# A weight maximum's matmul moved behind its diagonal, in a fused attention and two-layer expert kernel

## The chip, the cores and the metric

The kernel runs on one core of a Trainium2 chip. Its engines work in parallel, each through its own queue in a fixed order: TensorE (PE, matmuls), VectorE (DVE), ScalarE (ACT), GpSimd (POOL) and SyncE (SP, which issues most DMA transfers). They meet by semaphores. The metric is the device time of one execution in microseconds (us), as the median of several runs. Traces come from one further execution under the hardware profiler.

## The reference

Attention without softmax, then two mixture-of-experts layers in which each token goes to one expert.

```python
scores = (1 / S) * z @ z.T            # 4 batches, S = 2496, 64 features
x = u * (np.maximum(scores, 0) ** 2 @ v)          # 9984 tokens of 256

logits = x @ w_gate                   # 8 experts
e_idx = argmax(logits);  gate_w = softmax(logits)[e_idx]
for e in range(8):                    # first layer; eom = sigmoid(x @ w_output_gate)
    y[mask_e] = gate_w * eom[:, e] * (np.maximum(x[mask_e] @ w1[e], 0) @ w2[e])   # hidden 1024
# the second layer: the same with weights of its own and without eom
```

All of it is float32 at the interface.

## The kernel before

The kernel multiplies in float16 with two parts a number: a high part, and a low part that holds what the high part lost. A product is then three matmuls. Every weight matrix must be scaled by a power of two near its largest magnitude and split before it can be used. There are 32 weight matrices of 1 MB (two a layer and expert). The 16 of the first layer are split during attention, the 16 of the second layer during the first expert layer, and that is where the change is.

**The expert layer.** Tokens were scattered into regions by expert. The layer works on 85 tiles (slots) of 128 tokens. Its program is a list `order` of 170 items, written out when the program is built: `g1` items (first matrix and Relu, for one half of a pair of slots) and `g2` items (second matrix, for one slot). In the steady part a g1 and a g2 alternate. I call an item a step, and count from 0; from step 16 on the even ones are g1, the odd ones g2.

- `g1` (L1279): 24 matmuls into a PSUM tile `hp`; ACT does the Relu into the high part of the buffer HB (L1303), DVE makes HB's low part (L1304). There are two `hp` tiles, used in turn.
- `g2` (L1306): 24 matmuls into a PSUM tile `yp`; there are two of these too. `post1` (L1332) then takes the row maximum on DVE (`gm`, L1345) and a scale from it (`yg`), ACT makes the scaled high part (L1347), and DVE the low part (`rowb`, L1350). Every four slots the routing for the second layer follows in some twenty short DVE instructions and four scatters on POOL.

**The weights of the second layer.** `weight_pieces(..., offload=True)` (L392) returns a list of small pieces. From step 31 on, the end of a step takes the next piece; in the first steps it takes two, so that the list lasts exactly to the last of these steps (L1626 to L1631). A matrix has these pieces:

- `p0`, `p1`: the largest magnitude of the first and second half of the matrix, a DVE reduction of 128x1024 each (L427, L430). `p1` also puts the 128 partitions' maxima on a diagonal, `wd` (L436).
- `p1b`: appends the diagonal to the queue `wmq`. The next g2 takes it out and multiplies it by a matrix of ones (`wm_mm`, L384). The product stands in unused columns of that g2's `yp` tile and has all 128 maxima in every partition.
- `first`: `p2s` reduces that product to the maximum (`wy`, L450) and makes the scale `ws`. Then ACT scales half of the matrix in place and makes its high part (`phi`, L463 and L464), and POOL subtracts for the low part (`plo`, L471).
- `last`: `phi` and `plo` of the other half.
- `flush`: POOL issues the stores of the split halves (L477) and the load of the matrix after the next one (L402). There are two load buffers, `wstB`.

There are seven pieces a matrix, some of them empty, so a matrix takes seven steps, and the pieces of successive matrices fall on g1 and g2 in turn. The order on each engine is that in which this Python code calls the instructions; no scheduler changes it.

Of the kernel before, what the change touches and what calls it, by code (L numbers as in the profile page):

```python
# [27 lines left out]
def kernel(  # L28
# [15 lines left out]
    P = 128  # L44
    B, S, D = u.shape
# [334 lines left out]
        return pieces  # L380

    wmq = deque()

    def wm_mm(dst):  # L384
        st, dg = wmq.popleft()
        st["wm"] = dst
        T.matmul(dst, onesb, dg, start=True, stop=True)

# [3 lines left out]
    def weight_pieces(items, wst, wo, eng, offload):  # L392
        pend = []

        def flush():
            while pend:
                pend.pop(0)()
# [8 lines left out]
        def mk(k):  # L406
            i, e = items[k]
            w = wst[k % 2]
            st = {}
# [19 lines left out]
            def p1():  # L429
                V.tensor_reduce(st["m"][:, 1:2], w[:, H:], axis=AX.X, op=ALU.max, apply_absolute_value=True)  # L430
                if offload:
                    m1 = sm.tile([P, 1], F32, name=f"wx{i}_{e}", tag="wx")
                    dg = sm.tile([P, P], BF16, name=f"wd{i}_{e}", tag="fd", bufs=1)
                    tt(m1, st["m"][:, 0:1], st["m"][:, 1:2], ALU.max)
                    V.tensor_single_scalar(m1.bitcast(I32), m1.bitcast(I32), EXPM, ALU.bitwise_and)
                    V.tensor_scalar(dg, idn, m1, None, ALU.mult)  # L436
                    st["dg"] = dg
                    return
                st["m2"] = sm.tile([P, 2], F32, name=f"wr{i}_{e}", tag="wr")
                GP.partition_all_reduce(st["m2"], st["m"], P, bass.bass_isa.ReduceOp.max)  # L440

            def p1b():
                wmq.append((st, st["dg"]))

            def p2s():
                m1 = sm.tile([P, 1], F32, name=f"wy{i}_{e}", tag="wy")
# [49 lines left out]
                pass  # L496

            if offload:
                return (p0, p1, none, p1b, none, first, last)
            return (p0, p1), (p2s, lambda: phi(0), lambda: plo(0)), (lambda: phi(1), lambda: plo(1))  # L500

        ms = [mk(k) for k in range(len(items))]

        none = (0.0, lambda: None)
        if offload:
            pieces = [(0.0, lambda: w_load(0)), none, none, (0.0, lambda: w_load(1)), none]
            for m in ms:
                pieces += [(0.0, flush)] + [(0.0, f) for f in m]
                pieces[-len(m) - 1 : -len(m) + 1] = [(0.0, lambda p0=m[0]: (flush(), p0()))]
            return pieces + [(0.0, flush)]  # L510

        cost = (1.14, 1.14), (0.8, 0.67, 1.2), (0.67, 1.2)

# [3 lines left out]
        pieces = [(0.0, lambda: w_load(0)), none, none, none] + part(0, 0) + [(0.0, lambda: w_load(1)), none]  # L517
        for k in range(len(items)):
            last = part(k, 2)
# [786 lines left out]
    def g2(m, s):  # L1306
        e = eoff2.pop((m, s))
        i, h, _ = hslot.pop((m, s))
        hfree.append((i, h))
        yp = ps.tile([P, 512], F32, name=f"yp{m}_{s}", tag="a")  # L1310
        if wmq:
            wm_mm(yp[:, D : D + P])
        for f in range(FC):
            rh = wreg(e, arena0 + W2O + f * 4 * D)
            rl = wreg(e, arena0 + W2O + f * 4 * D + 2 * D)
            hi = T.lower_ap(HB[i][:, 0, f, h * P : h * P + P], for_matmul_weights=True)
            lo = T.lower_ap(HB[i][:, 1, f, h * P : h * P + P], for_matmul_weights=True)
            mm_reg(yp[:, :D], hi, reg_ap(rh, D, W2F), f == 0, False)
            mm_reg(yp[:, :D], hi, reg_ap(rl, D, W2F), False, False)
            mm_reg(yp[:, :D], lo, reg_ap(rh, D, W2F), False, f == FC - 1)  # L1320
        return yp

    lgq = deque()
# [229 lines left out]
    for m in range(2):  # L1553
# [42 lines left out]
        touched2 = False  # L1596
        for at, o in enumerate(order):
            kind, s = o[:2]
            if wload:
                wload.popleft()()  # L1600
            if kind == "g1":
# [73 lines left out]
```

## Time and profile before

| | |
|---|---|
| median of 3 runs (lowest to highest) | 1708.35 us (1705.81 to 1709.58) |
| the profiled execution | 1695.75 us |
| its span, first to last instruction | 1693.9 us |
| PE busy | 1627.4 us, 96% of the span |
| DVE busy | 1103.2 us, 65% |
| ACT busy | 934.2 us, 55% |
| POOL busy | 391.4 us, 23% |
| mean granted PE clock | 0.988 of full speed |

An instruction is busy from its start to its end. A time of idleness stands with the instruction that ended it, together with what released that instruction ("<-DVE wd L436": the semaphore came from DVE's instruction on `wd`, line 436). Engines other than the one that decides may be idle at no cost. The granted clock is given as a share of 2.4 GHz; its other level is half of that.

Attention ends some 700 us into the span. The first expert layer's steps follow (its first hp matmul starts at 704.0 us), the part with the weight pieces being from about 800 to 1160 us, and the second expert layer runs from about 1230 us to the end.

### The profile page before, as it was taken

The page shows a single profiled execution, that of the slowest core. Times are in us where ns is not written, and L with a number is a line of the kernel's source. Part 1 is how long each engine was busy: PE and PEld are TensorE (multiplying, and loading weights), DVE is VectorE, ACT ScalarE, POOL GpSimd, SP SyncE. Part 2 cuts the span into 40 slices and gives each one's busy share as a digit, 9 for nine tenths or more (in the row PEclk, how much of TensorE's full clock was granted, in tenths as well). Part 3 has the DMA queues.
Part 4 walks back from the last instruction along what each step waited for, and adds up shares of the span by engine and source line. Part 5 has one row for each costly group of instructions (what it writes and reads, how often), then busy time and mean ns, then how long its engine had stood idle before and what let it go on. Part 6 is the DMA issues. An engine that isn't in the chain of part 4 may idle for free. (4 is left out here: it accounts for less than half of the span.)

```text
span 1693.9 us, 41656 instructions
## 1 busy us (share of the span) xinstructions
PE 1627.4 (96%) x15668; PEld 1350.4 (80%) x15668; DVE 1103.2 (65%) x2805; ACT 934.2 (55%) x1082; POOL 391.4 (23%) x385
## 2 busy tenths in 40 slices
PE   8999999999999999989899899889989999999998
PEld 6777677767776777778788778789878888889997
DVE  8799899989999898656666766675463222222221
ACT  8898899889988998422344344443132222222221
POOL 1011111121111221111344344443121111111113
PEclk9999999999999999999999999999999999999999
DMA  5441643363534446962685568653892222222210
GB/s 147 122 110 44 192 101 90 115 202 101 133 99 143 140 138 183 286 167 62 179 186 167 159 157 175 159 141 87 248 275 60 67 51 51 51 51 52 52 33 30
DMA packets 289518, 212.05 MB, mean 125 GB/s; under 512 B 232297, under 2 KB 261358, under 8 KB 284976
## 3 DMA queue, kind: packets, MB, share of 16 engines
q1 hardware_dynamic: 268432, 144.51, 35.5%
q0 software_dynamic: 20896, 64.89, 11.6%
q8 instruction: 134, 2.20, 0.5%
q14 instruction: 56, 0.46, 0.1%
HBM read 92.80 MB, written 69.30 MB: 96 GB/s over the span
## 5 line engine op out<-in xcount | busy, mean ns | idle before, releaser
L1041 PEld LDWEIGHTS <-p 128*128 128x128 f16 (+1 forms) x4644 | 443.8, 98 | 105.3 <-issue 40.2
L1151 PE MATMUL yp<-W2R,HB 128*128 x4080 | 485.4, 278 | 0.1
L1151 PE MATMUL hp<-xt,W1R 128*128 128x256 f16 (+1 forms) x5088 | 475.4, 252 | 9.4 <-DMA xt<-region 3.9
L1151 PEld LDWEIGHTS <-HB 128*128 128x128 f16 x4080 | 403.8, 100 | 88.7 <-issue 36.4
L1304 DVE SCALAR_TENSOR_TENSOR HB<-hp,HB 128x1024 f16<-128x1024 f32 x170 | 207.8, 1223 | 385.2 <-ACT HB L1303 384.8
L1151 PEld LDWEIGHTS <-W1R 128*128 x5088 | 413.0, 98 | 46.1 <-issue 7.0
L1303 ACT ACTIVATE HB<-hp 128x1024 f16<-128x1024 f32 x170 | 173.4, 1021 | 246.3 <-PE hp L1151 236.4
L1041 PE MATMUL acc<-vhA,p 128*128 128x256 f16 (+1 forms) x2322 | 271.1, 273 | 3.6 <-DVE p L151 1.6
L1041 PE MATMUL acc<-vhB,p 128*128 128x256 f16 (+1 forms) x2322 | 270.6, 273 | 0.6 <-ACT acs L1051 0.6
L151 DVE TENSOR_TENSOR p<-r,p 128x1024 f16<-128x1024 f32 (+4 forms) x260 | 244.7, 954 | 36.6 <-ACT p L1006 33.8
L998 ACT ACTIVATE r<-s 128x1024 f32<-128x1024 f32 (+1 forms) x200 | 198.7, 994 | 56.2 <-PE s L987 48.0
L999 ACT ACTIVATE r<-r 128x1024 f32<-128x1024 f32 (+1 forms) x200 | 207.2, 1036 | 6.4
L654 POOL DMA_INDIRECT region<-rowb,pi x80 | 100.1, 1252 | 399.2 <-DVE pi L645 380.9
L1006 ACT ACTIVATE p<-r 128x1024 f16<-128x1024 f32 (+1 forms) x180 | 186.3, 1035 | 5.1
L1442 POOL DMA_INDIRECT out_dram<-rowb,oi x85 | 83.5, 983 | 348.0 <-ACT rowb L1441 342.4
L1347 ACT ACTIVATE rowb<-yp,yg 128x256 f16<-128x256 f32 x85 | 40.1, 472 | 223.2 <-DVE yg L167 187.4
L654 POOL DMA_INDIRECT region<-rowb,piq x85 | 85.0, 1000 | 208.3 <-DVE piq L641 64.7
L1441 ACT ACTIVATE rowb<-yp,cs 128x256 f32<-128x256 f32 x85 | 40.3, 474 | 143.2 <-PE yp L1151 136.3
L471 POOL TENSOR_TENSOR woB<-wstB,woB 128x1024 f16<-128x1024 f32 x32 | 68.1, 2133 | 100.6 <-ACT woB L464 100.5
L1350 DVE SCALAR_TENSOR_TENSOR rowb<-yp,yg,rowb 128x256 f16<-128x256 f32 x85 | 41.1, 483 | 54.5 <-ACT rowb L1347 53.8
L1345 DVE TENSOR_REDUCE gm<-yp 128x1 f32<-128x256 f32 x85 | 35.5, 418 | 27.5 <-PE yp L1151 27.4
L463 ACT ACTIVATE wstB<-wstB,ws 128x1024 f32<-128x1024 f32 x32 | 36.6, 1143 | 30.1 <-DVE ws L457 30.1
(266 smaller groups left out, 1159.1 us busy)
## 6 DMA issues: line engine op xcount, KB each, us to landing
wstA<-in_moe_w_dram SPq DMA_DIRECT2D x16, 1024.0 KB
wsplit<-woA SPq DMA_DIRECT2D x32, 512.0 KB
W1R<-wsplit SPq DMA_DIRECT2D x16, 1024.0 KB
W2R<-wsplit SPq DMA_DIRECT2D x16, 1024.0 KB
wstB<-in_moe_w_dram POOLq DMA_DIRECT2D x16, 1024.0 KB, 8.9
wsplit<-woB POOLq DMA_DIRECT2D x32, 512.0 KB, 4.8
u<-in_u_dram SPq DMA_DIRECT2D x16, 512.0 KB
vraw<-in_v_dram SPq DMA_DIRECT2D x3, 2432.0 KB
```

The source lines that it names most:

```text
L151: V.tensor_tensor(o, a, b, op)
L471: GP.tensor_tensor(lo, src, hi, ALU.subtract)
L654: d = GP.indirect_dma_start(reg[m], bass.IndirectOffsetOnAxis(ap=posi[:r, t : t + 1], axis=0), rows[:r, t, :], None, bounds_check=NROW - 1 ...
L998: A.activation(r[:, :, :W], s[:, :, :W], AF.Relu)
L999: A.activation(r[:, :, :W], r[:, :, :W], AF.Square, scale=2.0)
L1006: A.activation(p[:, 0, :, :W], r[:, :, :W], AF.Copy)
L1041: T.matmul(o, l, r, start=first and i == 0, stop=j == NT - 1 and i == len(mms) - 1, skip_group_check=True,)
L1151: T.add_instruction(mybir.InstMatmult(name=nc.get_next_instruction_name(), ins=[rhs, lhsT], outs=[T.lower_ap(o)], start_tensor_calc=start, ...
L1303: A.activation(hv, hpv, AF.Relu)
L1304: V.scalar_tensor_tensor(lv, hpv, 0.0, hv, ALU.max, ALU.subtract)
L1350: V.scalar_tensor_tensor(r16[:, q, D : 2 * D], yp[:, :D], yg, r16[:, q, :D], ALU.mult, ALU.subtract)
L1442: d = GP.indirect_dma_start(out, bass.IndirectOffsetOnAxis(ap=ot[:, q : q + 1], axis=0), y, None, bounds_check=N - 1, oob_is_err=False,)
```

## The change

```diff
--- before.py
+++ after.py
@@ -380,9 +380,10 @@
         return pieces
 
     wmq = deque()
+    at_item = [0]
 
     def wm_mm(dst):
-        st, dg = wmq.popleft()
+        _, st, dg = wmq.popleft()
         st["wm"] = dst
         T.matmul(dst, onesb, dg, start=True, stop=True)
 
@@ -434,13 +435,10 @@
                     tt(m1, st["m"][:, 0:1], st["m"][:, 1:2], ALU.max)
                     V.tensor_single_scalar(m1.bitcast(I32), m1.bitcast(I32), EXPM, ALU.bitwise_and)
                     V.tensor_scalar(dg, idn, m1, None, ALU.mult)
-                    st["dg"] = dg
+                    wmq.append((at_item[0] + 4, st, dg))
                     return
                 st["m2"] = sm.tile([P, 2], F32, name=f"wr{i}_{e}", tag="wr")
                 GP.partition_all_reduce(st["m2"], st["m"], P, bass.bass_isa.ReduceOp.max)
-
-            def p1b():
-                wmq.append((st, st["dg"]))
 
             def p2s():
                 m1 = sm.tile([P, 1], F32, name=f"wy{i}_{e}", tag="wy")
@@ -496,7 +494,7 @@
                 pass
 
             if offload:
-                return (p0, p1, none, p1b, none, first, last)
+                return (p0, p1, none, none, none, none, first, last)
             return (p0, p1), (p2s, lambda: phi(0), lambda: plo(0)), (lambda: phi(1), lambda: plo(1))
 
         ms = [mk(k) for k in range(len(items))]
@@ -504,10 +502,14 @@
         none = (0.0, lambda: None)
         if offload:
             pieces = [(0.0, lambda: w_load(0)), none, none, (0.0, lambda: w_load(1)), none]
-            for m in ms:
-                pieces += [(0.0, flush)] + [(0.0, f) for f in m]
-                pieces[-len(m) - 1 : -len(m) + 1] = [(0.0, lambda p0=m[0]: (flush(), p0()))]
-            return pieces + [(0.0, flush)]
+            steps = [list(m[:7]) for m in ms] + [[]]
+            for k, m in enumerate(ms):
+                steps[k][1] = lambda p1=m[1]: (flush(), p1())
+                if k:
+                    steps[k][0] = lambda lo=ms[k - 1][7], p0=m[0]: (p0(), lo())
+                steps[k] = [(0.0, f) for f in steps[k]]
+                pieces += steps[k]
+            return pieces + [(0.0, ms[-1][7]), (0.0, flush)]
 
         cost = (1.14, 1.14), (0.8, 0.67, 1.2), (0.67, 1.2)
 
@@ -1308,8 +1310,6 @@
         i, h, _ = hslot.pop((m, s))
         hfree.append((i, h))
         yp = ps.tile([P, 512], F32, name=f"yp{m}_{s}", tag="a")
-        if wmq:
-            wm_mm(yp[:, D : D + P])
         for f in range(FC):
             rh = wreg(e, arena0 + W2O + f * 4 * D)
             rl = wreg(e, arena0 + W2O + f * 4 * D + 2 * D)
@@ -1318,6 +1318,8 @@
             mm_reg(yp[:, :D], hi, reg_ap(rh, D, W2F), f == 0, False)
             mm_reg(yp[:, :D], hi, reg_ap(rl, D, W2F), False, False)
             mm_reg(yp[:, :D], lo, reg_ap(rh, D, W2F), False, f == FC - 1)
+        if wmq and at_item[0] >= wmq[0][0]:
+            wm_mm(yp[:, D : D + P])
         return yp
 
     lgq = deque()
@@ -1596,6 +1598,7 @@
         touched2 = False
         for at, o in enumerate(order):
             kind, s = o[:2]
+            at_item[0] = at
             if wload:
                 wload.popleft()()
             if kind == "g1":
```

`p1b` is gone. `p1` itself queues the diagonal, with the number of the step plus four, and a g2 takes it only from that step on. The matmul is issued behind the 24 matmuls of that g2, not ahead of them. The pieces are put together differently: a matrix's `p0` now shares a piece with the `last` of the matrix before, and stands first in it; `flush` goes with `p1`. The list has 119 pieces for 118.

On PE, this is the multiplication for the sixth matrix (`wd2_5`: weight set 2, expert 5; its g2 is that of slot 33). Before:

```order
L1151 MATMUL hp0_36_1_13483<-xt0_36_12899,W1R_55 128x256
L387 LDWEIGHTS onesb_107
L387 MATMUL yp0_33_13546<-wd2_5_13420,onesb_107 128x128
L1151 LDWEIGHTS HB2_59
L1134 ISA
L1151 MATMUL yp0_33_13546<-W2R_56,HB2_59 128x256
```

and now:

```order
L1153 MATMUL yp0_33_13546<-W2R_56,HB2_59 128x256
L388 LDWEIGHTS onesb_107
L388 MATMUL yp0_33_13546<-wd2_5_13367,onesb_107 128x128
L550 LDWEIGHTS xlt_126
L550 MATMUL mbank0_156<-ghl_133,xlt_126 128x16
```

The same `yp` tile takes it, but behind the g2's last matmul. It is so for 15 of the 16 matrices. The first one's product goes to another bank (`mbank0`, which also holds router logits) at the end of the step whose g2 took it before, since its `first` comes before a g2 may take it.

On DVE, this is where the two maxima (`wm2_5`) and the diagonal (`wd2_5`) of the same matrix are made. Its `p1` used to follow a g1. Before:

```order
L1350 SCALAR_TENSOR_TENSOR rowb0_123<-yp0_31_13305,yg31_13346,rowb0_123 128x256
L614 TENSOR_REDUCE seq6_13355<-arq6_13246 128x4
L620 TENSOR_SCALAR seq6_13355<-seq6_13355 128x4
L621 RECIPROCAL seq6_13355<-seq6_13355 128x4
L151 TENSOR_TENSOR rowb2_125<-seq6_13355,kq6_13228 128x4
L427 TENSOR_REDUCE wm2_5_13363<-wstB1_87 128x1
L1304 SCALAR_TENSOR_TENSOR HB1_58<-hp0_36_0_13374,HB1_58 128x1024
L430 TENSOR_REDUCE wm2_5_13363<-wstB1_87 128x1
L151 TENSOR_TENSOR wx2_5_13419<-wm2_5_13363 128x1
L435 TENSOR_SCALAR wx2_5_13419<-wx2_5_13419 128x1
L436 TENSOR_SCALAR wd2_5_13420<-idn_110,wx2_5_13419 128x128
L1345 TENSOR_REDUCE gm8_13465<-yp0_32_13424 128x1
```

and now:

```order
L428 TENSOR_REDUCE wm2_5_13302<-wstB1_87 128x1
L1347 TENSOR_REDUCE gm7_12999<-yp0_31_13307 128x1
L167 TENSOR_SCALAR yg31_13348<-gm7_12999 128x1
L1352 SCALAR_TENSOR_TENSOR rowb0_123<-yp0_31_13307,yg31_13348,rowb0_123 128x256
L616 TENSOR_REDUCE seq6_13357<-arq6_13246 128x4
L622 TENSOR_SCALAR seq6_13357<-seq6_13357 128x4
L623 RECIPROCAL seq6_13357<-seq6_13357 128x4
L151 TENSOR_TENSOR rowb2_125<-seq6_13357,kq6_13228 128x4
L431 TENSOR_REDUCE wm2_5_13302<-wstB1_87 128x1
L151 TENSOR_TENSOR wx2_5_13366<-wm2_5_13302 128x1
L436 TENSOR_SCALAR wx2_5_13366<-wx2_5_13366 128x1
L437 TENSOR_SCALAR wd2_5_13367<-idn_110,wx2_5_13366 128x128
```

The first maximum has moved ahead of the row maximum of slot 31 (`gm7`), the second one and the diagonal ahead of the low part of HB for slot 36. For the matrix before it (`wm2_4`), whose `p1` used to follow a g2, it is the other way round. Before:

```order
L1304 SCALAR_TENSOR_TENSOR HB2_59<-hp0_32_0_12903,HB2_59 128x1024
L427 TENSOR_REDUCE wm2_4_12950<-wstB0_86 128x1
L1345 TENSOR_REDUCE gm7_12993<-yp0_28_12952 128x1
L167 TENSOR_SCALAR yg28_12994<-gm7_12993 128x1
L590 TENSOR_REDUCE toq5_13007<-ohq5_12776 128x8
L151 TENSOR_TENSOR oacc1_153<-oacc1_153,toq5_13007 128x8
L1350 SCALAR_TENSOR_TENSOR rowb0_123<-yp0_28_12952,yg28_12994,rowb0_123 128x256
L430 TENSOR_REDUCE wm2_4_12950<-wstB0_86 128x1
L151 TENSOR_TENSOR wx2_4_13012<-wm2_4_12950 128x1
L435 TENSOR_SCALAR wx2_4_13012<-wx2_4_13012 128x1
L436 TENSOR_SCALAR wd2_4_13013<-idn_110,wx2_4_13012 128x128
L1304 SCALAR_TENSOR_TENSOR HB2_59<-hp0_32_1_13017,HB2_59 128x1024
```

and now:

```order
L428 TENSOR_REDUCE wm2_4_12896<-wstB0_86 128x1
L1306 SCALAR_TENSOR_TENSOR HB2_59<-hp0_32_0_12905,HB2_59 128x1024
L431 TENSOR_REDUCE wm2_4_12896<-wstB0_86 128x1
L151 TENSOR_TENSOR wx2_4_12953<-wm2_4_12896 128x1
L436 TENSOR_SCALAR wx2_4_12953<-wx2_4_12953 128x1
L437 TENSOR_SCALAR wd2_4_12954<-idn_110,wx2_4_12953 128x128
L1347 TENSOR_REDUCE gm7_12999<-yp0_28_12958 128x1
```

Here the first maximum has moved ahead of HB for slot 32, and the second maximum and the diagonal ahead of the row maximum of slot 28. On ACT, POOL and SP the instructions stand in the same order as before.

## Rows read from the trace of the kernel before

**Rows 1.** Windows, the seven cycles: busy us of each engine, clock, DMA share, GB/s

```profile
836.90:1140.20 303.30, 275.90 (x2844) 245.17 (x2844) 209.66 (x605) 130.19 (x167) 138.27 (x133) 0.97 0.69 167
```

**Rows 2.** Waits of PE, 780 to 1190 us: total us, times, longest

```profile
PE yp L387 <- DVE wd L436: 30.1, 12, 4.3
```

**Rows 3.** Time line of PE: start us, us, line, tiles, [idle before <- what ended it]

```profile
836.90 0.22 PE L387 MATMUL yp<-wd,onesb 128*128 128x128 bf16 x1 [2.12 <-DVE wd L436]
...
878.90 0.22 PE L387 MATMUL yp<-wd,onesb 128*128 128x128 bf16 x1 [2.40 <-DVE wd L436]
...
901.14 0.22 PE L387 MATMUL yp<-wd,onesb 128*128 128x128 bf16 x1
...
920.90 0.22 PE L387 MATMUL yp<-wd,onesb 128*128 128x128 bf16 x1 [3.39 <-DVE wd L436]
...
1140.19 0.22 PE L387 MATMUL yp<-wd,onesb 128*128 128x128 bf16 x1 [3.60 <-DVE wd L436]
```

**Rows 4.** Windows behind waits of line 387; the last but two is PE's clock

```profile
816.00:822.00 6.00, 5.28 (x41) 4.12 (x41) 3.97 (x14) 1.40 (x3) 0.00 (x0) 0.72 0.41 69
...
1094.00:1101.00 7.00, 6.66 (x48) 5.06 (x48) 4.00 (x14) 1.86 (x3) 2.06 (x2) 0.55 0.52 146
...
1140.00:1147.00 7.00, 6.81 (x75) 5.78 (x75) 4.18 (x14) 1.86 (x3) 0.00 (x0) 0.76 0.29 30
```

**Rows 5.** Waits of DVE, 836.9 to 1140.2 us

```profile
DVE HB L1304 <- ACT HB L1303: 45.4, 27, 3.5
...
DVE rowb L1350 <- ACT rowb L1347: 35.1, 48, 2.2
```

**Rows 6.** Time line of DVE, waits behind ACT and a first maximum

```profile
852.85 1.23 DVE L1304 SCALAR_TENSOR_TENSOR HB<-hp,HB 128x1024 f16<-128x1024 f32 x1 [2.60 <-ACT HB L1303]
...
893.85 1.23 DVE L1304 SCALAR_TENSOR_TENSOR HB<-hp,HB 128x1024 f16<-128x1024 f32 x1 [0.83 <-ACT HB L1303]
...
911.85 1.23 DVE L1304 SCALAR_TENSOR_TENSOR HB<-hp,HB 128x1024 f16<-128x1024 f32 x1 [3.27 <-ACT HB L1303]
...
914.51 0.48 DVE L1350 SCALAR_TENSOR_TENSOR rowb<-yp,yg,rowb 128x256 f16<-128x256 f32 x1 [0.91 <-ACT rowb L1347]
...
916.67 1.21 DVE L427 TENSOR_REDUCE wm<-wstB 128x1 f32<-128x1024 f32 x1
```

**Rows 7.** Time line of ACT, two Relus

```profile
844.19 1.02 ACT L1303 ACTIVATE HB<-hp 128x1024 f16<-128x1024 f32 x1 [1.55 <-PE hp L1151]
...
910.81 1.01 ACT L1303 ACTIVATE HB<-hp 128x1024 f16<-128x1024 f32 x1
```

**Rows 8.** Time line of DVE, waits that end on PE: first and last

```profile
821.29 0.42 DVE L1345 TENSOR_REDUCE gm<-yp 128x1 f32<-128x256 f32 x1 [1.24 <-PE yp L1151]
...
1144.69 0.42 DVE L1345 TENSOR_REDUCE gm<-yp 128x1 f32<-128x256 f32 x1 [1.17 <-PE yp L1151]
...
845.25 1.23 DVE L1304 SCALAR_TENSOR_TENSOR HB<-hp,HB 128x1024 f16<-128x1024 f32 x1 [1.38 <-ACT HB L1303]
...
1148.66 1.22 DVE L1304 SCALAR_TENSOR_TENSOR HB<-hp,HB 128x1024 f16<-128x1024 f32 x1 [2.28 <-ACT HB L1303]
```

**Rows 9.** Line 436 (ns min/median/max), and time line of DVE and POOL

```profile
L436 DVE TENSOR_SCALAR wd<-idn,wx x16: 285/286/2762, 816.4 to 1139.9; 128x128 bf16<-128x128 f32 x16
...
834.08 2.76 DVE L436 TENSOR_SCALAR wd<-idn,wx 128x128 bf16<-128x128 f32 x1
...
834.61 2.14 POOL L471 TENSOR_TENSOR woB<-wstB,woB 128x1024 f16<-128x1024 f32 x1
...
914.20 2.12 POOL L471 TENSOR_TENSOR woB<-wstB,woB 128x1024 f16<-128x1024 f32 x1 [1.07 <-ACT woB L464]
```

**Rows 10.** Time line and line 402, a weight load and its reader

```profile
861.65 0.74 POOL L402 DMA_DIRECT2D wstB<-in_moe_w_dram  x1
...
873.93 1.21 DVE L427 TENSOR_REDUCE wm<-wstB 128x1 f32<-128x1024 f32 x1
...
DMA to landing us min/median/max: 7.1/8.9/11.2
```

## The prediction

> **What bounds the kernel now.** I read the views in this order: the page by engine, the waits of PE in the first expert layer, PE's time line around those waits, and then what VectorE (DVE) and ScalarE (ACT) do meanwhile. The sums stand on the stretch in which the second layer's weights are split beside the first layer's matmuls.
>
> In that stretch PE is the engine that should never stop, and it stops almost only for one thing: the 128x128 matmul that spreads a weight matrix's maximum over the partitions (line 387) waits for its diagonal, `wd`, 30.1 us in 12 of its 16 places [rows 2]. A matmul that waits holds all of PE, since the 24 matmuls of its g2 stand behind it. The waits come in pairs of matrices: at 878.90 it waited 2.40 us, at 901.14 not at all, at 920.90 3.39 us [rows 3]. I call the first kind A and the second B; seven steps a matrix and a g2 at every second step make them alternate.
>
> A wait also costs after its end. In the six us from 816.0 the granted clock is 0.72 of full speed, in the seven from 1094.0 0.55, in the seven from 1140.0 0.76 [rows 4]: after these stops PE ran for a while at 1.2 instead of 2.4 GHz. Time lost is length times (1 - clock): 6 x 0.28 = 1.7 us and 7 x 0.45 = 3.2 us. Dips of the first size are five in all, from the one at 816 to the one at 1140, and that at 1094 is the only long one, so 5 x 1.7 + 3.2 = 11.7 us.
>
> The obvious sum is therefore 30.1 + 11.7 = 41.8 us. I do not take it, and the reason is the next view. From the wait at 836.90 to the one at 1140.19 are 303.3 us, seven cycles of an A and a B [rows 3]. DVE is busy for 209.7 us of it [rows 1] and waits 45.4 us for ACT's Relu and 35.1 us for ACT's scaled copy [rows 5], which with smaller waits leaves it next to no free time. DVE and ACT hand work to each other in a fixed order: DVE takes the row maximum, ACT scales, DVE makes the low part, ACT does the Relu, DVE makes its low part. That chain, not PE, may be what fills the cycle. So the question is how long it is when PE no longer stops.
>
> **The chain's length.** A wait of DVE is free time only where PE was late. HB at 845.25 waited 1.38 us, and there ACT itself had been idle 1.55 us for the hp matmuls [rows 7, 8]: PE's doing. HB at 911.85 waited 3.27 us, but the Relu before it started at 910.81 without a gap, right behind two ACT passes that split a weight half [rows 6, 7]: the chain's own. Sorted so, DVE waited for PE from 816 to 1150 in six row maxima (1.24, 0.34, 1.13, 0.27, 1.53 and 1.17 us) and eight HB steps (1.38, 1.00, 1.20, 2.22, 1.38, 0.33, 1.87 and 2.28 us), of which the first and the last stand in [rows 8]: 5.7 + 11.7 = 17.4 us. One cycle shows the two engines against each other: 42.0 us from 878.90 to 920.90 [rows 3], where PE stopped 3.39 us and so needs 38.6, while DVE has one such wait of 1.00 us in the same 42.0 and needs 41.0.
>
> **The change part by part.**
> - The matmul goes from the start of a g2 to its end; for 15 of the 16 matrices it is the same g2. The matrix's two maxima and its diagonal move one step forward on DVE. Each step is some 2.7 us (38.6 / 14), so the diagonal gets about two steps, 5.4 us, more. The longest wait is 4.3 us [rows 2], so the waits at this line go: -30.1 us, and the dips that follow them with them. For the first matrix the matmul goes to another bank behind the g2 that took it, and holds it no longer.
> - What is late next: DVE's chain. PE may run ahead of it until a PSUM tile is not yet read, two tiles of a kind deep. Then PE waits for HB (L1304) or for the low part (L1350). A dip of PE's clock costs little there, because PE waits for DVE anyway. So the gain is what the chain gives up, not the 41.8 us.
> - First part of it: its waits for PE, 17.4 us, as PE is ahead now.
> - Second part: the first maximum (1.21 us at 916.67 [rows 6]) now stands before a step for which DVE waits on ACT, and fills that wait. For B these are HB's waits behind the second weight half: 2.60 us at 852.85, 0.83 at 893.85 [rows 6], and over the seven cycles 2.60 three times, 0.83 twice, and twice none. Filled: 3 x 1.2 + 2 x 0.8 = 5.3 us. For A the maximum stands ahead of the row maximum; the copy's wait at 914.51, 0.91 us [rows 6], has some 0.54 us of hand-over that stays, so 0.4 is filled there and 0.3 in two others: 0.9 us. The rest of it only changes place. Together 6.2 us.
> - The instructions of ACT, GpSimd (POOL) and the DMA queues stand in the same order as before, so stores and loads are issued where they were. But the maximum that reads a loaded matrix comes one step earlier. The tightest load was issued at 861.65 and read at 873.93, 12.3 us; without a step it is 9.6, against 7.1 to 11.2 us from issue to landing [rows 10]. Cost 0 to 1.6 us there, and in a second place like it; I take 0, the median being 8.9.
> - One matmul more or less is not in it: 16 stay 16, at 0.22 us each [rows 3]. The row maximum of those g2's may wait for it: 16 x 0.2 = 3 us at most on DVE; I take 0, because DVE is behind PE there. There is one piece more in the list (119 for 118); one more step takes two pieces, and the last split ends at the same step.
>
> **Where a rule speaks against it.** The diagonal at 834.08 took 2.76 us, and ended with a subtraction on GpSimd that began at 834.61 and took 2.14, where the median of the sixteen is 0.29 [rows 9]; one other was as long. The Trainium skill (SBUF — State Buffer, "SBUF: two separate sides") says why: VectorE and GpSimd share a port pair as an exclusive lock, and the loser waits for the whole instruction. The trace agrees in these two places of sixteen. By that rule a diagonal nearer to the subtraction could be caught in every matrix; that is a rival below, worked out from the rows alone.
>
> **Sum.** 17.4 + 6.2 = 23.6 us. It is made against the profiled execution, 1695.75 us (span 1693.9 and 1.85 around it). The runs' median, 1708.35, lies 12.6 us higher, and I take the difference to stay: 1708.35 - 23.6 = 1684.8, say 1685 us. What comes behind (the loads of the second layer's weights, and all of the second layer) starts earlier by as much; nothing in it has a fixed time.
>
> **Rivals.**
> - PE becomes the bound again: DVE catches up in the freed places and PE neither stops nor dips. -41.8 us, 1667 us. For it: through the B matrices PE does not stop at all in the trace. Against: the 41.0 against 38.6 us of the cycle above.
> - The order buys nothing: the maximum ahead of the row maximum delays ACT's copy and the Relu behind it. That costs up to 1.2 us in each of 8 A matrices, 9.7 us, and the 6.2 us are not had: 17.4 - 9.7 = 7.7 us gained, 1701 us. For it: at A the wait that it could fill was only 0.91 us.
> - The lock, and this is the one that ends slower: in its new place every diagonal starts while GpSimd subtracts, and is held 2.76 - 0.29 = 2.5 us. Fourteen more of them lengthen the chain by 35 us: 23.6 - 35 = -11, 1720 us. It outweighs the gain from ten newly caught ones on. Against: at A in the trace the subtraction (2.12 us from 914.20 [rows 9]) ends before the first maximum at 916.67 [rows 6] starts, and another maximum (1.2 us) stands between it and the diagonal in either order.
> - The change does not do what it says: DVE falls so far behind that the matmul at g2's end finds no diagonal either, and the stop is the old one at another place: 1708 us. Against: the 5.4 us.
>
> **How the numbers follow.** Forecast (the chain takes over) 0.55; PE bound again 0.23; the order buys nothing 0.14; the lock 0.04; no effect 0.04. A measurement of this kernel can tell some 0.2% (3.4 us) from no change. The first three are faster, 0.92, of which I move 0.01 to the same for the third one's edge. Same: 0.04 + 0.01 = 0.05. Slower: 0.04. The range has PE bound again at its lower end with 3 us for the runs' spread, and the third case at its upper: 1664 to 1701 us. The likeliest case alone, with a load or lock here and there, is 1677 to 1692.
>
> **What would show it.** Line 387's wait on `wd` (now line 388) under 3 us in all. In its place waits of PE's hp and yp matmuls on DVE's HB, low part or weight scale, 10 to 20 us between 800 and 1150. Granted clock of the stretch still under 1.00. The spacing of the A matrices' diagonals near 40.5 us instead of 43.3 (303.3 / 7). DVE's waits for PE nearly gone. Wrong would be: PE without stops in that stretch (first rival), diagonals of over 2 us in most matrices (the lock), or a wait at line 388 of over 10 us.

## The result, and the profile after

The changed kernel took 1684.87 us (median of 4 runs, 1679.71 to 1690.63) beside 1708.10 us for the kernel before. The ratio is 0.9866, with a 95% interval of 0.9823 to 0.9909, so 22.9 us less (15.5 to 30.2). The forecast was 1685 us.

The kernel before had a median of 1708.1 us in this group of runs and of 1695.1, 1695.9 and 1703.2 us in the three groups of experiments, each of which ran on another chip. So ratios are compared across groups, not times. The profiled execution of the kernel before (1695.75 us) is of the size of the first two groups of experiments; the changed kernel's first one (span 1688.7 us) is the longest of its four. The changed kernel was therefore run and profiled once more in the first group of experiments, and this trace (span 1668.1 us against 1693.9, so 25.8 us shorter) stands beside the one of before below. I call it the second trace.

First, what PE waits for between 780 and 1190 us: total us, times, longest. In the first trace of the changed kernel:

```profile
PE hp L1153 <- issue: 8.4, 16, 1.2
PE mbank L550 <- DVE Lq L555: 6.0, 5, 2.3
PE mbank L746 <- DVE mpa L739: 3.1, 1, 3.1
PE mbank L550 <- DMA xlt<-rowb: 2.5, 1, 2.5
PE yp L1153 <- issue: 2.5, 4, 1.3
PE hp L1153 <- DVE HB L1306: 2.4, 3, 1.0
...
PE yp L1153 <- DVE rowb L1352: 0.6, 1, 0.6
```

and in the second:

```profile
PE mbank L550 <- DVE Lq L555: 7.4, 4, 2.4
PE mbank L550 <- DMA xlt<-rowb: 4.8, 5, 1.9
PE hp L1153 <- DVE HB L1306: 3.6, 2, 2.8
PE mbank L746 <- DVE mpa L738: 3.3, 1, 3.3
...
PE yp L1153 <- DVE rowb L1352: 0.6, 1, 0.6
```

The 30.1 us at the multiplication of the maximum [rows 2] are gone: no row of either trace names `wd`. In their place PE waits for DVE 12.1 us (6.0 + 3.1 + 2.4 + 0.6) in these rows of the first and 14.9 us (7.4 + 3.6 + 3.3 + 0.6) in the second, and 2.5 and 4.8 us for a transfer. Line 550 makes the router's logits of the second layer: its matmuls wait until DVE has read (`Lq`, L555) the logits of the group before, or until the transposed rows (`xlt`) have landed. Line 746 is a matmul for the second layer's table of tiles. The rows that end on "issue" are gaps that nothing in the profile releases; at `hp` and `yp` they are long only in the first trace, and they come back in the last section.

The windows of the second trace answer to [rows 1] and [rows 4]: length, busy us of PE, PEld, DVE, ACT and POOL, PE's clock, DMA share, GB/s. The first row holds the seven cycles, the second the longest stop of PE (3.3 us) and what stands behind it, the last the stretch between the first layer's first hp matmul and the cycles.

```profile
829.00:1118.20 289.20, 272.52 (x2847) 243.16 (x2845) 207.63 (x607) 130.80 (x169) 141.00 (x135) 0.98 0.75 176
...
1068.00:1078.00 10.00, 6.69 (x45) 4.53 (x42) 8.39 (x27) 2.78 (x4) 2.70 (x4) 0.66 0.73 224
...
702.80:829.00 126.20, 120.43 (x1185) 107.43 (x1185) 80.32 (x262) 37.36 (x51) 23.53 (x26) 1.00 0.60 156
```

Seven cycles take 289.2 us for 303.3, so 41.3 us each for 43.3. DVE is idle 289.2 - 207.6 = 81.6 us in them, for 303.3 - 209.7 = 93.6: 12.0 of the 14.1 us gained are idle time of DVE. Which idle time, the waits of DVE in the same stretch show (answering to [rows 5]):

```profile
DVE HB L1306 <- ACT HB L1305: 31.8, 23, 3.3
DVE rowb L1352 <- ACT rowb L1349: 29.7, 46, 2.2
DVE wm L428 <- DMA wstB<-in_moe_w_dram: 5.9, 3, 3.7
DVE rowb L1352 <- DMA me<-region: 2.2, 1, 2.2
DVE rowb L1352 <- DMA region<-rowb,piq: 2.2, 1, 2.2
```

By these rows the two waits behind ACT lost 13.6 and 5.4 us, and 10.3 us of waits for transfers stand there now. The last two rows are in truth ACT's. A wait is put down to what came last by the profile, but here ACT's scaled copy ended just before DVE went on, as the time lines of ACT and DVE show for one of them (start us, us, [idle before <- what ended it]); the other, at 919.88, is alike:

```profile
880.35 0.46 ACT L1349 ACTIVATE rowb<-yp,yg 128x256 f16<-128x256 f32 x1
...
880.84 0.48 DVE L1352 SCALAR_TENSOR_TENSOR rowb<-yp,yg,rowb 128x256 f16<-128x256 f32 x1 [2.20 <-DMA me<-region]
```

Read so, the waits behind ACT fell from 81.1 us (45.4 + 35.1 [rows 5], and 0.6 of the same kind) to 65.9 (31.8 + 29.7 + 2.2 + 2.2), by 15.2 us. Waits for PE's `yp`, 3.3 us before, are gone, and 5.9 us of waits for weight loads are new. And ACT itself waits less for PE's `hp`: from 780 to 1190 us it was 37.3 us before, and now it is

```profile
ACT HB L1305 <- PE hp L1153: 23.2, 13, 4.9
```

The remaining gain lies outside the seven cycles. The starts of PE's first `hp` matmul of each layer and of the multiplications split the two spans like this (us; a multiplication now stands behind its g2 and not ahead, so the two pieces beside the cycles are shifted by a g2 against each other, and their sum is the safer number):

| stretch | before | second trace | less |
|---|---|---|---|
| start to the first layer's first hp | 704.0 | 702.9 | 1.1 |
| to the second multiplication | 132.9 | 126.2 | 6.7 |
| seven cycles | 303.3 | 289.1 | 14.2 |
| to the second layer's first hp | 92.9 | 88.4 | 4.5 |
| to the end | 460.8 | 461.5 | -0.7 |

In the second of these stretches the clock was not full before, as its window shows,

```profile
704.00:836.80 132.80, 122.80 (x1160) 107.21 (x1159) 82.80 (x263) 37.35 (x51) 26.30 (x28) 0.96 0.57 151
```

but part of that has nothing to do with the change. In both traces PE stops there, before the first weight piece, for the load of `W2R` (3.15 us before, 3.27 in the second trace). Behind this stop the clock was low before and full in the second trace. The same window, before and in the second trace:

```profile
736.00:742.00 6.00, 6.00 (x30) 4.15 (x29) 0.68 (x4) 0.07 (x1) 0.00 (x0) 0.51 0.70 222
...
736.00:742.00 6.00, 6.00 (x57) 5.38 (x56) 3.58 (x17) 0.95 (x2) 0.00 (x0) 1.00 0.59 175
```

The same window has 0.72 in the first trace of the changed kernel and 0.53 in that of `e1_matmul_at_end` below. So some 6 x 0.49 = 2.9 us of the 6.7 us, and of the 25.8, is a difference between two executions.

DVE has long waits for PE beside the cycles. In the second trace, from 1118.1 to 1206.6 us:

```profile
DVE gm L1347 <- PE yp L1153: 10.2, 12, 4.5
```

Last, the diagonal, whose 2.76 us spoke for a lock [rows 9] (ns min/median/max, starts):

```profile
L437 DVE TENSOR_SCALAR wd<-idn,wx x16: 286/288/411, 812.6 to 1115.8; 128x128 bf16<-128x128 f32 x16
```

None of the sixteen is held. The two that were held before (2.76 and 2.63 us) are short now.

### The profile page after: what moved, and what is told of

Same layout as the page of the kernel before. It is cut to its first block, busy times and chain, and to the rows that moved or that the text cites. A ratio compares the mean times of both kernels' runs of the same rounds, so it can differ in the third digit from the quotient of the medians.

```text
span 1688.7 us, 41655 instructions
## 1 busy us (share of the span) xinstructions
PE 1626.6 (96%) x15668; PEld 1348.4 (80%) x15668; DVE 1096.4 (65%) x2805; ACT 933.8 (55%) x1082; POOL 391.3 (23%) x385
## 3 DMA queue, kind: packets, MB, share of 16 engines
q0 software_dynamic: 20896, 64.89, 12.1%
## 5 line engine op out<-in xcount | busy, mean ns | idle before, releaser
L1153 PE MATMUL hp<-xt,W1R 128*128 128x256 f16 (+1 forms) x5088 | 482.7, 253 | 16.4 <-issue 9.3
L1153 PE MATMUL yp<-W2R,HB 128*128 x4080 | 474.4, 274 | 4.2 <-issue 3.5
L1153 PEld LDWEIGHTS <-W1R 128*128 x5088 | 416.1, 99 | 58.4 <-issue 19.6
L1153 PEld LDWEIGHTS <-HB 128*128 128x128 f16 x4080 | 398.1, 98 | 56.7 <-issue 10.1
L461 ACT ACTIVATE wstB<-wstB,ws 128x1024 f32<-128x1024 f32 x32 | 36.6, 1143 | 30.6 <-DVE ws L455 26.5
```

The source lines that it names most:

```text
L1153: T.add_instruction(mybir.InstMatmult(name=nc.get_next_instruction_name(), ins=[rhs, lhsT], outs=[T.lower_ap(o)], start_tensor_calc=start, ...
```

## The experiments

Theory 1 in the expectations: once PE does not stop at `wd`, the chain of DVE and ACT sets the pace, and PE's new waits are its symptom. Theory 2: PE is bound itself, and what is missing to its 41.8 us (ratio 0.9755) is lost elsewhere. All ratios are to the kernel before on the same chip, with 95% intervals.

### One part alone: the matmul's place, or the order of the maxima

`e1_matmul_at_end` is the kernel before with only this:

```diff
-        if wmq:
-            wm_mm(yp[:, D : D + P])
         for f in range(FC):
...
+        if wmq:
+            wm_mm(yp[:, D : D + P])
         return yp
```

> The kernel before with one edit: the matmul stands behind the g2's 24 matmuls; the maxima and the diagonal stay where they were. Theory 1 (the chain of DVE and ACT sets the pace once PE is released): each wait at the matmul has one step, 2.7 us, less, so of 30.1 us some 6 us stay; the chain loses its waits for PE but fills no wait of its own, so some 12 to 17 us faster than before (ratio about 0.992). Theory 2 (PE itself is the bound once it is released, and what is missing from 41.8 us lies in loads and in PE's own gaps): about as fast as the changed kernel less the 6 us, 16 to 20 us faster, and no new waits of PE on DVE.

0.9919 (0.9898 to 0.9940), 1682.92 us for 1695.09. Its waits of PE, 780 to 1190 us:

```profile
PE yp L387 <- DVE wd L436: 9.3, 8, 2.5
PE mbank L548 <- DVE Lq L553: 8.2, 6, 1.8
```

A g2 later, two thirds of the waits for `wd` are gone, and 13.7 us with them. PE waits on DVE at other places as well.

`e2_maxima_early` is the changed kernel with the multiplication back at the g2's start:

```diff
         yp = ps.tile([P, 512], F32, name=f"yp{m}_{s}", tag="a")
+        if wmq and at_item[0] >= wmq[0][0]:
+            wm_mm(yp[:, D : D + P])
         for f in range(FC):
...
-        if wmq and at_item[0] >= wmq[0][0]:
-            wm_mm(yp[:, D : D + P])
         return yp
```

> The changed kernel with one edit: the matmul stands ahead of the g2's 24 matmuls again; the maxima and the diagonal are a step earlier, as changed. Theory 1: the waits at the matmul are again cut by one step only, some 6 us stay; the first maximum fills waits of DVE behind ACT (6 us), so 15 to 23 us faster than before, near the changed kernel and some 5 us ahead of the run with the matmul at the end alone. Theory 2: the same time as that run, since only the diagonal's slack counts.

0.9877 (0.9855 to 0.9900). Waits of PE, 780 to 1190 us; it waits for `wd` in as many places as e1:

```profile
PE yp L388 <- DVE wd L437: 8.8, 7, 1.7
...
PE mbank L388 <- DVE wd L437: 2.1, 1, 2.1
```

and is 0.0042, 7.1 us, faster than e1. So the time differs while PE's waits at this matmul do not (10.9 for 9.3 us): the new order shortens the chain. The two intervals just touch, but all five runs of e2 (1674.40 to 1679.12 us) lie below all six of e1 (1680.34 to 1686.26), on one chip. What the order shortens is not only the wait behind ACT. In e1 two diagonals are still held at over 2.6 us, as before the change, and in e2 none is. The sixteen diagonals of e1 and of e2 (busy us, mean ns):

```profile
L436 DVE TENSOR_SCALAR wd<-idn,wx 128x128 bf16<-128x128 f32 x16 | 9.4, 588 | 0.6
...
L437 DVE TENSOR_SCALAR wd<-idn,wx 128x128 bf16<-128x128 f32 x16 | 5.0, 312 | 0.6
```

That is 4.4 us less work of DVE, and the longest wait of e1 for `wd`, 2.5 us at 836.10, stands behind a held one. No run tells this part of the 7.1 us from the filled waits. On top of the order the matmul's place adds 0.0010 or 1.7 us (`e4_changed_again` below), which is not to be told from nothing.

### The changed kernel again, and with less work on DVE

`e4_changed_again` has no edit; it gave the second trace.

> The changed kernel as it is, for its ratio in more rounds on the same chip and for a second trace of it. Theory 1 and theory 2 alike: 0.9866 within its interval. If the idle time of PE that nothing released (12.8 us in the first trace) is that execution's own, it is different here, and the span with it by about as much.

0.9867 (0.9843 to 0.9891): 1672.83 us for 1695.09. The ratio is that of the first group.

`e3_short_maxima` takes the second layer's scale from an eighth of each half:

```diff
-                V.tensor_reduce(st["m"][:, 0:1], w[:, :H], axis=AX.X, op=ALU.max, apply_absolute_value=True)
+                V.tensor_reduce(st["m"][:, 0:1], w[:, : (H // 8 if offload else H)], axis=AX.X, op=ALU.max, apply_absolute_value=True)
...
-                V.tensor_reduce(st["m"][:, 1:2], w[:, H:], axis=AX.X, op=ALU.max, apply_absolute_value=True)
+                V.tensor_reduce(st["m"][:, 1:2], w[:, H : (H + H // 8 if offload else 2 * H)], axis=AX.X, op=ALU.max, apply_absolute_value=True)
```

> The changed kernel, but the two maxima of a matrix are taken over an eighth of each half (so the scale comes from a sample): DVE has about 16 x 2 x 1.0 = 32 us less to do between 800 and 1150 us. Theory 1: the chain is then shorter than PE's 38.6 us a cycle, PE becomes the bound, and the kernel is 10 to 18 us faster than the changed one, near 1667 us; PE's waits on DVE go from 12 us to under 4. Theory 2: within 4 us of the changed kernel.

0.9785 (0.9762 to 0.9807), 13.9 us below the changed kernel by the ratios, and the intervals are apart. The group of the first maximum, 780 to 1190 us, in the second trace (busy us, mean ns | idle before)

```profile
L428 DVE TENSOR_REDUCE wm<-wstB 128x1 f32<-128x1024 f32 x16 | 19.4, 1213 | 8.7 <-DMA wstB<-in_moe_w_dram 8.7
```

and here

```profile
L428 DVE TENSOR_REDUCE wm<-wstB 128x1 f32<-128x128 f32 x16 | 4.5, 279 | 4.5 <-DMA wstB<-in_moe_w_dram 4.5
```

with as much at the second maximum (19.4 and 4.4 us), show 29.9 us less work of DVE, on no other engine. With it PE waits for DVE only 5.2 us in the same stretch,

```profile
PE hp L1153 <- DVE HB L1306: 2.6, 1, 2.6
PE mbank L550 <- DVE Lq L555: 2.0, 1, 2.0
...
PE mbank L746 <- DVE mpa L738: 0.6, 1, 0.6
```

and DVE waits for PE, by its own waits, 10.7 us for 4.4:

```profile
DVE gm L1347 <- PE yp L1153: 10.7, 12, 2.9
```

So in the changed kernel DVE's work was on the path (theory 1), and the new bound, 0.9785, is near the 0.9755 that I gave for a PE without stops.

### The weight loads

`e5_load_with_last` issues a matrix's stores, and the load behind them, a step earlier:

```diff
-                steps[k][1] = lambda p1=m[1]: (flush(), p1())
                 if k:
-                    steps[k][0] = lambda lo=ms[k - 1][7], p0=m[0]: (p0(), lo())
+                    steps[k][0] = lambda lo=ms[k - 1][7], p0=m[0]: (p0(), lo(), flush())
```

> The changed kernel, but the stores and the next load are issued in the same piece as the last subtraction, a step earlier on GpSimd's queue. In the traces of the changed kernel DVE waits 9 to 12 us in 4 places for a weight load, which I had taken as 0. Theory 1 (the chain of DVE and ACT sets the pace): these waits lengthen the chain; where scatters stood between subtraction and load the load comes 5 to 10 us earlier, the waits fall to some 5 us, and the kernel is 2 to 6 us faster than the changed one (ratio to before about 0.984). Theory 2 (the waits lie in free time of DVE): within 2 us of the changed kernel.

0.9867 (0.9837 to 0.9898): nothing gained. DVE's wait for loads hardly changed (8.7 us in the second trace):

```profile
DVE wm L428 <- DMA wstB<-in_moe_w_dram: 8.5, 2, 5.7
```

`e7_load_halves` is e5 with each load in two DMAs:

```diff
-            eng.dma_start(
...
+            for h in range(2 if offload else 1):
+                r = slice(h * n // 2, (h + 1) * n // 2) if offload else slice(0, n)
+                eng.dma_start(dst[:, r], src[:, r])
```

> As the run with the load moved, and the load is made in two halves, of which the first maximum needs only the first. Theory 1: DVE's waits for loads go to under 2 us, 6 to 11 us faster than the changed kernel (ratio to before about 0.982). Theory 2: no more than 2 us.

0.9853 (0.9826 to 0.9881), and the wait is 5.1 us shorter than in the second trace:

```profile
DVE wm L430 <- DMA wstB<-in_moe_w_dram: 3.6, 2, 1.8
```

By the ratios that is 2.4 us less than the changed kernel, within its interval. Theory 1 had it that these waits count in full; 5 us of them taken away bought less than half, if anything.

### Where PE meets the chain: the router's logits

`e8_logits_two_banks` lets every second group's logits of the second router go to another PSUM bank:

```diff
+        if kind == "lg" and lgalt[0] and i % 2:
+            return mbank[1][:, 320:384]
...
+                lgalt[0] = True
                 gr["lg"] = mslot("lg")
+                lgalt[0] = False
```

> The changed kernel, but every other group of the second router's logits goes to the other small PSUM bank. In the changed kernel PE waits 6 to 7 us for DVE to read the logits of the group before, at matmuls of the next group. Theory 1: that wait is only the place at which PE meets the chain's lag; it goes, and PE waits as long at hp, yp or the other bank, so the time is within 2 us of the changed kernel. Rival: the shared bank itself costs the 6 us; then it is 4 to 7 us faster.

0.9953 (0.9936 to 0.9970): slower than the changed kernel by 0.0086, 14.6 us, which neither theory had. The waits of PE:

```profile
PE mbank L553 <- DVE t3q L151: 18.2, 5, 7.5
...
PE mbank L553 <- DVE Lq L558: 1.0, 1, 1.0
```

`mbank[1]` also holds, in other columns, what DVE reads for `t3q` late in a group's routing. The logits' matmul now waits for that read, up to 7.5 us, with all of PE behind it. So a wait of PE for DVE is not always a harmless symptom: it costs where it comes earlier than the chain's own limit. The Trainium skill (PSUM — Partial Sum Buffer, "PSUM bank collisions raise a hardware error") says that the compiler's scheduler ties any two instructions on different engines that touch the same bank and quadrant; this trace shows such a tie, with its 18.2 us, but no run shows which program set it here.

`e11_logits_later` leaves the bank and issues these logits a step later:

```diff
-        lgq.append((clk[0] + LGD[s >= LATE], lgt))
+        lgq.append((clk[0] + LGD[s >= LATE] + (2.6 if q == 0 and s < LATE else 0.0), lgt))
```

> The changed kernel, but the first slot's router logits of each group are issued one step later on PE (slots before the last part), so PE meets the bank that DVE must have read one step later. Theory 1 (the chain of DVE and ACT is full and sets the pace wherever PE meets it): the 6 to 7 us of waits at the logits go and come back at hp and yp; within 3 us of the changed kernel. Rival (two steps of lead are too few, and DVE idles later for PE because of it): 4 to 7 us faster (ratio to before about 0.983).

0.9872 (0.9843 to 0.9901), not faster, though the wait for `Lq` fell from 6.0 and 7.4 us in the two traces to

```profile
PE mbank L550 <- DVE Lq L555: 0.6, 1, 0.6
```

Here it is a symptom: without it PE waits elsewhere or nowhere, and the end does not move.

`e12_halves_logits_later` joins the edits of e7 and e11.

> The run with the load in halves and issued earlier, and the logits one step later. Theory 1: as the run with the halves, ratio to before 0.985 within 0.001. Rival: both gains add, 6 to 9 us faster than the changed kernel, ratio about 0.982.

0.9835 (0.9805 to 0.9864), 1675.18 us for 1703.17: the lowest ratio of a version with all of the computation, but the intervals of the changed kernel and of e7 overlap with it. That it is faster is not shown.

`e13_short_maxima_too` adds e3's edit to that (the scale is again taken from an eighth).

> As the run before in this list, with the maxima over an eighth of each half (the scale comes from a sample). Theory 1: DVE's part of the chain is shorter by some 32 us, PE is the bound and its waits between 780 and 1190 us fall to 10 us or less; ratio to before 0.974 to 0.979, at or below the run with the short maxima alone. Rival (PE is held by other things than DVE's work): as the changed kernel with halves, 0.984.

0.9837 (0.9805 to 0.9870), where 0.974 to 0.979 was expected; its runs lie between 1661.98 and 1679.69 us. So e3's edit gained nothing here that can be told from nothing, where it gained 13.9 us above. Inconclusive: the trace is of the fastest one, with PE waiting for DVE in five places, 3.0 us in all, so it doesn't show what held the others. Part of it is the clock: the fastest run has a mean granted clock of 0.998, the others 0.992 to 0.994, which over 1660 us makes, as an estimate, 7 to 10 of the 9 to 18 us between them.

### ACT's share

`e9_one_act_pass` takes one of ACT's two passes per half away and gives the scaling to POOL:

```diff
-                    A.activation(src, src, AF.Copy, scale=st["sc"])
-                    A.activation(hi, src, AF.Copy)
+                    A.activation(hi, src, AF.Copy, scale=st["sc"])
...
+                    GP.tensor_scalar(src, src, st["sc"], None, ALU.mult)
                     GP.tensor_tensor(lo, src, hi, ALU.subtract)
```

> The changed kernel, but ACT makes the high part straight from the loaded weights with the scale, and GpSimd scales them in place ahead of its subtraction: 32 ACT passes of 1.14 us go, GpSimd gets 32 passes more. Theory 1 (the chain of DVE and ACT together): DVE's waits of 3.3 us behind two ACT passes go to some 2.2, the chain loses 20 to 30 us, PE becomes the bound, 8 to 14 us faster than the changed kernel (ratio to before about 0.980). Rival (DVE's own work alone is what PE meets): within 4 us. If GpSimd holds DVE at the ports they share, diagonals and scales of over 1 us show it.

0.9938 (0.9915 to 0.9960): 0.0071 or 12 us slower than the changed kernel. It says little of ACT, since POOL's pass is long and DVE pays for it. POOL's new group from 780 to 1190 us (busy us, mean ns), and the window of that stretch:

```profile
L468 POOL TENSOR_SCALAR wstB<-wstB,ws 128x1024 f32<-128x1024 f32 x32 | 91.1, 2847 | 48.9 <-ACT woB L461 48.6
...
780.00:1190.00 410.00, 381.36 (x4159) 342.84 (x4158) 295.18 (x815) 135.22 (x185) 262.06 (x197) 0.98 0.69 157
```

POOL is busy for 262.1 us, 174.5 in the second trace, and DVE for 295.2 us with 815 instructions, where the second trace has 280.3 with 838. PE waits for `wd` again in four places, 4.0 us, and DVE for the loads, whose issue stands behind POOL's pass, 15.6 us. The rule of the prediction on the port that VectorE and GpSimd share (the Trainium skill, SBUF — State Buffer, "SBUF: two separate sides") agrees in part with what is seen here. Five diagonals took 0.87 to 1.91 us. Two of them, at 874.22 and 972.28, ended with a pass of POOL that was under way. The other three, the longest (1908 ns) among them, ended 1.2 us into such a pass, so they did not wait for the whole instruction.

`e14_no_act_scaling` leaves the scaling out altogether, without POOL's pass; the low parts of the second layer's weights are then wrong.

> The changed kernel, but ACT's pass that scales the weights in place is left out and the high part is made with the scale straight from the loaded weights (the low parts of the second layer's weights are then wrong); GpSimd has no pass more. Theory 1 (ACT's passes are part of the chain): 32 x 1.14 = 36 us less on ACT, DVE's waits of 3.3 us behind two passes go to 2.2, 7 to 14 us faster than the changed kernel (ratio about 0.980). Rival (DVE's own work alone sets the pace): within 3 us.

0.9822 (0.9793 to 0.9851): 1672.38 us, 9.4 us below e11 on the same chip (all six runs, 1671.07 to 1675.67, lie below all six of e11, 1678.42 to 1683.62), and 0.0045 or 7.6 us below the changed kernel's ratio. The pass removed is this one of the second trace:

```profile
L461 ACT ACTIVATE wstB<-wstB,ws 128x1024 f32<-128x1024 f32 x32 | 36.6, 1143 | 29.9 <-DVE ws L455 28.8 <-DVE winv L170 1.1
```

The longest wait of DVE behind ACT's scaled copy is halved, from 2.2 us (waits of DVE of e14):

```profile
DVE rowb L1351 <- ACT rowb L1348: 34.0, 64, 1.1
```

ACT, 42% busy in the stretch, is on the path too: 36.6 us less of its work is worth 9.4 us beside e11, and 7.6 us by the ratio to the changed kernel, whose interval overlaps a little; 29.9 us less of DVE's was worth 13.9. The edit also lets POOL's subtraction start a pass earlier, which no run tells apart.

## Why the prediction was right

**The amount.** 23.6 us were forecast; 22.9 were timed and the second trace is 25.8 us shorter. The reason given holds: the stops at `wd` are gone and PE's own sum of 41.8 us was not had, because DVE and ACT set the pace. e3 shows DVE's part by taking work from it alone, and e14 ACT's. The first rival, PE bound again, is refuted by both: a kernel that PE bounds gains nothing from them. In the last group of experiments e13 does not repeat what e3 showed, and that stays open.

That the sum came out within 2.2 us is in part luck. It had too much in the cycles and too little beside them, it left out two things that pull in opposite directions (the loads, and the diagonals that were held), and 2.9 us of the second trace's gain is a clock that the change does not touch. Each comes below.

**Its two terms.** The 17.4 us (DVE's waits for PE) and the 6.2 us (the first maximum in a wait behind ACT) were not measured one by one, but e1 and e2 come near: 13.7 us for the matmul's place, with 9.3 us of waits left, and 7.1 us more for the order, of which up to 4.4 can be the held diagonals. The rival "the order buys nothing" (7.7 us in all) falls with that. Both parts take from the same waits: behind the order, the place gives 1.7 us, without it 13.7.

**Where it lies: off.** The step "PE waits for HB or for the low part" named the wrong place. These two make 4.2 of the 14.9 us; the most, 7.4, is a logits matmul. The time line of DVE in the second trace (start us, us, [idle before <- what ended it]) shows why:

```profile
941.82 1.23 DVE L1306 SCALAR_TENSOR_TENSOR HB<-hp,HB 128x1024 f16<-128x1024 f32 x1 [3.27 <-ACT HB L1305]
942.96 1.21 DVE L428 TENSOR_REDUCE wm<-wstB 128x1 f32<-128x1024 f32 x1
944.09 0.41 DVE L1347 TENSOR_REDUCE gm<-yp 128x1 f32<-128x256 f32 x1
...
945.23 0.48 DVE L1352 SCALAR_TENSOR_TENSOR rowb<-yp,yg,rowb 128x256 f16<-128x256 f32 x1 [0.54 <-ACT rowb L1349]
945.63 0.21 DVE L555 TENSOR_REDUCE Lq<-mbank 128x32 f32<-128x64 f32 x1
```

and that of PE beside it:

```profile
945.90 0.24 PE L550 MATMUL mbank<-ghl,xlt 128*128 128x16 f16 x4 [1.74 <-DVE Lq L555]
```

DVE waits 3.27 us for ACT, does a low part, a maximum, a row maximum and a low part, and only then the sum `Lq` that frees the bank of the logits. `hp` and `yp` have two tiles, the logits one (its three places in the bank are guarded as one), so PE meets the chain there first. I counted the buffers of two kinds of tile and not of the third.

**The cycle: 41.3 us, not 40.5.** Seven cycles gave 14.2 us where 7 x 2.8 = 19.6 were forecast, and the stretches beside them 11.2 where 4 were left. In the cycles DVE's waits for ACT and for PE fell by 15.2 + 3.3 = 18.5 us, about the 20.7 that seven eighths of 23.6 make, but the waits for weight loads, taken as nothing, came to 5.9 us. Beside the cycles, where DVE waits for PE up to 4.5 us, a stop of PE counts with its clock. Ahead of them stood stops of 2.34 and 2.12 us, and the clock went from 0.96 to 1.00. Of the 11.2 us, 2.9 are the dip at 736 us that the change does not touch; 8.3 are left, still twice the 4. I saw that the sum of 41.8 is wrong in the cycles and did not ask whether it is right outside them. (A step of 38.6 / 14 is 2.8 us and not 2.7; nothing hangs on it.)

**The load waits: mis-sized.** I took 0 with an upper bound of two times 1.6 us. DVE waits for loads 8.7 us (second trace) and 11.7 (first), for 2.6 before. The longest stands in the first trace; POOL's time line has the issue,

```profile
999.94 0.92 POOL L403 DMA_DIRECT2D wstB<-in_moe_w_dram  x1
```

and DVE's the reader:

```profile
1014.28 1.22 DVE L428 TENSOR_REDUCE wm<-wstB 128x1 f32<-128x1024 f32 x1 [5.69 <-DMA wstB<-in_moe_w_dram]
```

From issue to reader it is 14.3 us, longer than any landing of before (11.2 [rows 10]). But by e5 and e7 the price is small, 2.4 us as measured and not to be told from nothing, so the error hardly reached the sum. How a wait of DVE of 5.7 us can cost so little isn't settled: the waits behind ACT would have to be shorter after it. The trace of e7 speaks for that, without showing it: with 5.1 us less of waits for loads, DVE's waits for HB behind ACT are 58.1 us, 56.5 in the second trace.

**The lock and no effect.** Neither came: no diagonal over 411 ns, no wait for `wd`. The lock was counted only as a risk, though, and the change took away the two holds that there were: 4.4 us of DVE's work (9.4 to 5.0 us for the sixteen diagonals) that the sum did not have. **The clock** stays under 1.00, as said (0.98 in the cycles). The longest dip left in the cycles is 0.66 over ten us, with the stop of 3.3 us in them.

## What to carry to other kernels

When the bound engine's waits go, look first at how much idle time the next chain has to give, engine by engine, and take that and not the waits; but do it stretch by stretch, because where the chain has slack, a stop counts in full. Before a gain is put down to the change, look for dips of the clock behind stops that both traces have. Then list every buffer through which the freed engine can run into the chain, with its depth: it will stop at the shallowest, and sharing that bank with a later reader (e8) costs more than the stop. A wait that is seen is priced only by taking it away: 6 us at the logits were worth nothing, and 5 us at the loads hardly more.

## What the runs showed of the hardware

In one set of traces PE has short gaps that no engine, transfer or semaphore of the profile ends. In 780 to 1190 us they make 12.8 us in the first trace of the changed kernel and 9.2 to 11.2 us in those of e11 to e14, but 0.6 us before and 0.8 to 4.0 us in e1 to e9. At `hp` and `yp` alone it is 10.9 and 8.2 to 9.3 us against 0.3 to 0.6. They come with the group of runs, not with the kernel: the same kernel has 12.8 us of them in one trace and 2.4 in the other. The medians of the kernel before are higher in those groups as well (1708.1 and 1703.2 for 1695.1 and 1695.9). What the gaps are is open, and so is whether they belong to a chip or to a time, since each group of experiments ran on another chip.

A scaling of 128x1024 fp32 in place took POOL 2847 ns, 2.5 times ACT's 1143, and with 32 of them DVE was busy 14.9 us longer in the stretch, with 23 instructions fewer. That cost does not show in one kind of instruction: the diagonals took 590 ns on average in e9, but 588 in the kernel before as well.

The same stop of PE, some 3.2 us for the load of `W2R`, was followed by a clock of 0.51 over six us in the trace of before and of 1.00 in the second trace, though the two programs first differ some 60 us later.
